# Attention, gated products and soft routing on one core: the first score products over 128 rows, with 20 identity products ahead of them

## The chip, the cores and the metric

The kernel runs on one core of a Trainium2 chip. The metric is device time in microseconds (us) of one execution; smaller is better. The comparison is the median of several executions of the kernel before with the same of the changed kernel. One execution of the kernel before was taken with the hardware profiler, and all rows below come from that one.

## The reference, cut to what matters

Three stages follow one another. Attention for 4 x 8 = 32 heads of 576 positions and width 64, with a decay bias and a causal mask; a gated product over the 2304 tokens; and soft routing of all tokens to 32 slots of 8 experts.

```python
scores = q @ k.T / sqrt(64)
bias   = -(cum[:, None] - cum[None, :])          # cum = cumsum(max(s, 0))
scores = where(causal, -1e9, scores + minimum(bias, 0))
x      = softmax(scores) @ v                     # heads side by side: 2304 x 512
g      = ((x @ w1) * (x @ w2)) @ w3 @ w_out      # 2304 x 512
logits = g @ phi                                 # 2304 x 32
# softmax over tokens -> slot inputs -> two expert layers -> softmax over slots -> out
```

The weights w1, w2, w3 and w_out are in float64, and the kernel turns them into float32 from their raw words.

## The kernel before, in words

A head's scores are products of a q tile and a k tile. The rows that are contracted are the 64 of the head plus 4 that carry the decay bias (two parts of the cumulative sum times ones), 68 in all. `ITEMS` has 40 entries: items 0 to 7 are the query tiles 0, 1, 2 (64, 128 and 128 queries, against 64, 192 and 320 keys) of heads 0 to 7, items 8 to 15 the query tiles 3 and 4 of the same heads (448 and 576 keys, the latter in two cuts of 288), and items 16 to 39 all five tiles of heads 8 to 31. `NF32 = 16` items are the first kind: their q and k stand in one float32 tile [128, 2, 576], rows 0 to 63 fetched by `att_fetch`, rows 64 to 67 by `att_prep` (for items 0 and 1 out of the tiles `dec`, L304, for the others out of the scratch `rows_d` in DRAM, L306), and one float32 product over `rows[:68]` (L308) makes a score tile. Each such product is two TensorE instructions with their weight loads. The later items split q and k into a high part and a rest and make two products of the float32r type, one over 128 rows (`qa`), one over 68 (`qb[:68]`).

The tiles of the first 16 items take turns in six places: three tags (`raw`, `qa`, `qb`) of `NRW = 2` buffers each, so item n takes the place of item n - 6.

For each item: scores in `att_scores` (L341 on TensorE, mask and row maximum on VectorE at L344, exponential on ScalarE at L349), `att_norm` (reciprocal on VectorE, multiplication on GpSimd at L362), `att_transpose` (transposes on TensorE at L377 and L391, copies on ScalarE), and for each pair of heads `att_pv` (products with v, `x_ps`, issued through the helper at L110). `glu_half` (L439, `gl`) makes the gated products over the finished columns of x. Between these steps the float64 words are fetched (L178) and converted (L186 to L201, and GpSimd at L218), three buffers deep.

The program's steps are woven by hand (`att_steps`, `weave`). SyncE issues nearly all DMAs, strictly in the order written. On the other engines a planner with a model of time (`schedule_with_timeline_sim=True`, L1114) puts the instructions in order when the program is built; on the chip each engine then runs its own order and waits on semaphores. `att_values` (L290) fetches v for a pair of heads into one of two buffers, so it waits until an earlier pair's `x_ps` products have read theirs, and every later fetch of SyncE stands behind it. `ident` is the 128 x 128 identity, made by GpSimd (`make_identity`, L747).

Of the kernel before, what the change touches and what calls it, by code (L numbers as in the profile page):

```python
# [10 lines left out]
F32 = mybir.dt.float32  # L11
# [10 lines left out]
P = 128  # L22
B, H, S, D = 4, 8, 576, 64
# [24 lines left out]
def attn_glu_softmoe_kernel(  # L48
# [14 lines left out]
    nc = tc.nc  # L63
# [16 lines left out]
    def psum(tag, name):  # L80
        return ps.tile([P, 512], F32, tag=tag, name=name, bufs=PB[tag])
# [3 lines left out]
    NRW, SCB, PTB, QAB, VB = 2, 3, 2, 2, 2  # L85
    NF32, NDIR, ND, FAR = 16, 2, 1, 3

    A1, CA, CB1, CB, GB1, GB, GC = 0.6, 8, 16, 26, 8, 16, 24

    LKS = {(0, 1): 8, (1, 0): 0, (1, 1): 4}  # L90

# [27 lines left out]
    ident = cp.tile([P, P], F32, name="ident")  # L119
# [144 lines left out]
    hd = {}  # L264
    ITEMS = [(h, t) for t in ((0, 1, 2), (3, 4)) for h in range(H)] + [(h, (0, 1, 2, 3, 4)) for h in range(H, NH)]

    def att_fetch(n, ap):
        h, tiles = ITEMS[n]
        if h % 2 == 0:
            b, c = divmod(h // 2, H // 2)  # L270
            for blk, (_, nt, own) in enumerate(BLK):
                if own[0] in tiles:
                    x_t[b, blk, c] = xpl.tile([P, 2, nt], F32R, tag=f"x{blk}", name=f"x_{b}_{blk}_{c}", bufs=NX)
        q0, q1 = QT[tiles[0]][0], sum(QT[tiles[-1]])
        tag = ("raw", "qa", "qb")[n % 3] if n < NF32 else "raw"
        raw = ap.tile([P, 2, S], F32, tag=tag, name=f"raw_{n}", bufs=NRW)
        m = 64 if n < NF32 else P
        if q0:
            nc.sync.dma_start(raw[:m, 0, q0:q1], qk[h, 0, :m, q0:q1])
            nc.sync.dma_start(raw[:m, 1, :q1], qk[h, 1, :m, :q1])  # L280
        else:
            nc.sync.dma_start(raw[:m, :, :q1], qk[h, :, :m, :q1].rearrange("n p t -> p n t"))
        hd[n] = dict(raw=raw, q0=q0, q1=q1)
# [9 lines left out]
    def att_prep(n, ap):  # L293
        h, tiles = ITEMS[n]
        t = hd[n]
        raw, q0, q1 = t["raw"], t["q0"], t["q1"]
        if n < NF32:
            rows = raw
        else:
            rows = ap.tile([P, 2, S], F32R, tag="qb", name=f"qb_{n}", bufs=QAB)  # L300
            qa = ap.tile([P, 2, S], F32R, tag="qa", name=f"qa_{n}", bufs=QAB)
        if n < NDIR:
            for a in range(2):
                nc.sync.dma_start(rows[64 + 2 * a : 66 + 2 * a, :, :q1].bitcast(F32), dec[a][h : h + 1, :, :, :q1])  # L304
        else:
            nc.sync.dma_start(rows[64:68, :, :q1].bitcast(F32), rows_d[h].rearrange("a b n t -> (a b) n t")[:, :, :q1])  # L306
        if n < NF32:
            t["mul"] = [rows[:68]]  # L308
            return
        rq, rk, qb = raw[:, 0], raw[:, 1], rows  # L310
        nc.vector.tensor_copy(qa[:, 0, q0:q1], rq[:, q0:q1])  # L311
        nc.scalar.dma_start(qb[0:64, 0, q0:q1].bitcast(F32), qa[0:64, 0, q0:q1].bitcast(F32))
        nc.vector.tensor_copy(qa[:, 1, :q1], rk[:, :q1])
        nc.gpsimd.tensor_tensor(  # L314
            out=qb[0:64, 1, :q1], in0=rk[0:64, :q1], in1=qa[0:64, 1, :q1].bitcast(F32), op=ALU.subtract
        )
        nc.gpsimd.tensor_tensor(  # L317
            out=qa[64:, 0, q0:q1], in0=rq[64:, q0:q1], in1=qa[64:, 0, q0:q1].bitcast(F32), op=ALU.subtract
        )
        t["mul"] = [qa, qb[:68]]  # L320

    def att_scores(n, i, ap):
        t, tiles = hd[n], ITEMS[n][1]
        if i == tiles[0]:
            t["nmax"] = sm.tile([P, 6], F32, tag="nmax", name=f"nmax_{n}")
            t["rsum"] = rsum_t[n % 3]
            if n >= H or n % 2 == 0:
                t["sc"] = ap.tile([P, 1600], F32, tag="sc", name=f"sc_{n}", bufs=SCB)
            else:
                t["sc"] = hd[n - 1]["sc"][:, 800:]  # L330
        nmax, rsum, mul = t["nmax"], t["rsum"], t["mul"]
        q0, r = QT[i]
        W = q0 + r

        r = P
        sc = t["sc"][:, 64 * i * i : 64 * i * i + W]
        cuts = [(0, W)] if W <= 512 else [(0, W // 2), (W // 2, W)]
        for m, (a, z) in enumerate(cuts):
            pp = psum("sg", f"sc_ps_{n}_{i}_{m}")
            for x in mul:  # L340
                nc.tensor.matmul(pp[:r, : z - a], x[:, 0, q0 : q0 + r], x[:, 1, a:z], start=x is mul[0], stop=x is mul[-1])  # L341
            m0 = S - P if i == 0 else S - W + a
            last = m == len(cuts) - 1
            nc.vector.tensor_tensor_reduce(  # L344
                out=sc[:r, a:z], in0=pp[:r, : z - a], in1=hd["mask"][:r, m0 : m0 + z - a], scale=-0.125,
                scalar=3.0e38 if m == 0 else nmax[:r, 5:6], op0=ALU.add, op1=ALU.min,
                accum_out=nmax[:r, i : i + 1] if last else nmax[:r, 5:6],
            )
        nc.scalar.activation(  # L349
            out=sc[:r, :W], in_=sc[:r, :W], func=AF.Exp, bias=nmax[:r, i : i + 1], scale=-1.0,  # L350
            accum_out=rsum[:r, i, 0:1],
        )
# [285 lines left out]
    def att_steps(ap):  # L638

        groups = [[] for _ in range(B + 1)]  # L640
        N = len(ITEMS)
        for n in range(N + 1):
            tiles = ITEMS[n][1] if n < N else ()
            old = [i for i in ITEMS[n - 1][1] if i] if 0 < n <= N else []
            sc = [(0.2 + 0.3 * i, lambda i=i, n=n: att_scores(n, i, ap)) for i in tiles]
            tr = [(0.2 + 0.3 * i, lambda i=i, n=n: att_transpose(n - 1, i, ap)) for i in old]
            norm = [(0, lambda n=n: att_norm(n - 1))] if 0 < n <= N else []
            prep = [(0, lambda n=n: att_values(n + 1, ap))] if n + 1 < N else []
            d = FAR if n + FAR < NF32 else 1 if NF32 <= n + 1 < N else 0
            if d:  # L650
                prep += [(0, lambda m=n + d: att_prep(m, ap))]
            d = FAR + 1 if n + FAR + 1 < NF32 else 2 if NF32 <= n + 2 < N else 0
            if d:
                prep += [(0, lambda m=n + d: att_fetch(m, ap))]
            blks = [k for k in range(2) if BLK[k][2][0] in ITEMS[n - 1][1]]
            pv = [(1.4, lambda n=n, k=k: att_pv(n - 2, k)) for k in blks] if n > 0 and n % 2 == 0 else []
            groups[min(B, max(0, (n - 1) // H))] += [
                *sc[:1], *norm, *sc[1:2], *prep, *sc[2:3], *tr[:1], *sc[3:4], *tr[1:2], *sc[4:], *tr[2:], *pv
            ]
        return groups  # L660
# [78 lines left out]
    with tc.tile_pool(name="att", bufs=1) as ap:  # L739
        phi_sb = ap.tile([P, KC, NS], F32, name="phi_sb")  # L740
        u_sb = ap.tile([P, FC, NS], F32, name="u_sb")
        decay_fetch()
        fetch_words(0, ap)
        att_fetch(0, ap)
        fetch_words(1, ap)
        att_fetch(1, ap)
        make_identity(nc, ident)  # L747
        mask = ap.tile([P, S], F32, name="mask")
# [9 lines left out]
        for n in range(NDIR):  # L758
            att_prep(n, ap)
# [4 lines left out]
        for n in range(NDIR, FAR):  # L764
            att_fetch(n + 1, ap)
            att_prep(n, ap)
# [36 lines left out]
        k = GC - GB  # L803
        steps = steps[GB:]
        run(weave(att[2], weave(steps[:k], prep[CB:]) + steps[k:]))
        for b in range(2, B):
            steps, late = glu_steps(b - 1, late)
            n = len(more) // (B - b)
# [5 lines left out]
    pp = pool("pp", 2, reuse_waits="tile")  # L814

    def big(where, name):
        if where == "w":
            return wp.tile([P, 2048], F32, tag="W", name=name, bufs=NW)
        if where == "t":
            return tp2.tile([P, 2048], F32, name=name)  # L820
        return ep.tile([P, 2048], F32, tag="E", name=name)
# [3 lines left out]
    for i in range(2):  # L825
        t = big("e", f"wo_t{i}").rearrange("p (i c) -> p i c", i=2)
# [3 lines left out]
    for i in range(4):  # L830
        t = big("e", f"w3_t{i}").rearrange("p (i c) -> p i c", i=2)
# [67 lines left out]
    for q in range(4):  # L899
        cols = slice(256 * q, 256 * q + 256)  # L900
        yps = psum(("acc", "sg")[q % 2], f"y_ps_{q}")
        for r in range(2):
            for j in range(4):
                f = 4 * r + j
                nc.tensor.matmul(  # L905
                    yps[32 * j : 32 * j + 32, :256], zt[:, j, NS * r : NS * r + NS], w3_t[f // 2][:, f % 2, cols],
                    start=r == 0, stop=r == 1,
# [7 lines left out]
    for r in range(2):  # L915
        for c in range(2):
            for j in range(4):
                f = 4 * r + j
                nc.tensor.matmul(
                    xp[c][32 * j : 32 * j + 32, :256], yt[:, f], wo_t[f // 4][:, f % 4, 256 * c : 256 * c + 256],  # L920
                    start=r == 0, stop=r == 1,
# [196 lines left out]
```

## Time and profile before

| what | value |
|---|---|
| median of 3 runs | 566.16 us (562.83 to 568.1) |
| the profiled execution, its own time | 565.44 us |
| span of that execution, first to last instruction | 563.6 us |
| mean granted TensorE clock over the span | 0.981 |
| TensorE busy (matmul) | 520.0 us, 92% |
| TensorE weight loads busy | 433.9 us, 77% |
| VectorE, ScalarE, GpSimd busy | 316.2, 310.0, 196.7 us |
| DMA, mean rate over the span | 209 GB/s |

The span is 1.84 us shorter than the execution's own time. PE is TensorE's matmul, PEld its weight load, DVE is VectorE, ACT ScalarE, POOL GpSimd, SP SyncE; SPq rows are DMA issues of SyncE's queue. The granted clock is a share of 2.4 GHz. Shares of busy time are means over stages of different kinds.

### The profile page before, as it was taken

Reading aid. Unit: us, or ns where it says so; the run is one execution under the profiler, and the core shown is the slowest. Engines: PE = TensorE matmul, PEld = TensorE weight load, DVE = VectorE, ACT = ScalarE, POOL = GpSimd, SP = SyncE. Lnnn points to the kernel's source line nnn. Section 1 sums busy time; section 2 is a strip of 40 time slices with the busy share of each in tenths; the row PEclk is TensorE's granted clock in tenths of the full one; section 3 lists DMA queues with packets and bytes.
Section 4 is the critical chain, followed back from the end, with each engine's and each line's share of the span. In section 5 each row is a group of like instructions: output and inputs, shape, how many; then the busy total and the mean of one; then the engine's idle time right before and its main releaser. Section 6 shows DMA issues by size and latency. Waiting matters only on the chain. (4 is left out here: it accounts for less than half of the span.)

```text
span 563.6 us, 11844 instructions
## 1 busy us (share of the span) xinstructions
PE 520.0 (92%) x4288; PEld 433.9 (77%) x4288; DVE 316.2 (56%) x966; ACT 310.0 (55%) x845; POOL 196.7 (35%) x247
## 2 busy tenths in 40 slices
PE   3789899998979999899899999999999999999993
PEld 2566688787768897889889889889988999853452
DVE  7568696889964385736574657446631311243333
ACT  4576586788865675646566567357833321321222
POOL 5475464438745374253354444333210000000000
PEclk9997899999979999999999999999999999999998
DMA  5765966868654173345646563555330999689977
GB/s 157 237 179 178 261 203 215 287 219 261 191 201 119 39 220 109 130 135 179 206 136 213 168 197 104 166 167 172 113 113 1 391 413 381 233 300 421 421 296 244
DMA packets 38809, 118.03 MB, mean 209 GB/s; under 512 B 4224, under 2 KB 10560, under 8 KB 35296
## 3 DMA queue, kind: packets, MB, share of 16 engines
q1 hardware_dynamic: 36832, 113.74, 58.8%
q10 hardware_dynamic: 1920, 3.54, 2.5%
q8 instruction: 34, 0.56, 0.4%
q14 instruction: 23, 0.19, 0.1%
HBM read 102.11 MB, written 11.60 MB: 202 GB/s over the span
## 5 line engine op out<-in xcount | busy, mean ns | idle before, releaser
L439 PE MATMUL gl<-x,w12t 128*128 128x320 f32 (+1 forms) x1536 | 238.3, 304 | 1.3 <-DVE nmax L344 0.7
L439 PEld LDWEIGHTS gl<-x,w12t 128*128 128x128 f32 x1536 | 212.2, 191 | 10.0 <-issue 4.3
L362 POOL TENSOR_SCALAR sc<-sc,rinv 128x64 f32<-128x64 f32 (+4 forms) x160 | 92.4, 594 | 53.9 <-DVE rinv L359 39.2
L349 ACT ACTIVATE sc<-sc,nmax 128x64 f32<-128x64 f32 (+4 forms) x160 | 89.5, 560 | 32.2 <-DVE nmax L344 31.6
L317 POOL TENSOR_TENSOR qa<-raw,qa 64x576 fp32r<-64x576 f32 x24 | 36.5, 1522 | 144.1 <-DVE qa L311 138.3
L344 DVE CUSTOM_DVE_ANT_0 sc<-sc_ps,mask 128x64 f32<-128x64 f32 (+4 forms) x160 | 64.8, 424 | 32.1 <-PE sc_ps L341 29.0
L379 ACT COPY pt<-pt_ps 128x128 f32<-128x128 f32 (+3 forms) x128 | 52.2, 423 | 27.1 <-PE pt_ps L377 16.3
L377 PE MATMUL pt_ps<-ident,sc 128*128 128x128 f32 x320 | 56.8, 288 | 4.9 <-ACT pt L379 2.3
L341 PE MATMUL sc_ps<-qa 128*128 128x64 f32 (+1 forms) x144 | 46.6, 336 | 6.0 <-DVE nmax L344 2.5
L377 PEld LDWEIGHTS pt_ps<-ident,sc 128*128 128x128 f32 x320 | 38.8, 145 | 17.3 <-issue 10.0
L341 PE MATMUL sc_ps<-qb 68*128 68x64 f32 (+1 forms) x144 | 44.2, 310 | 4.2 <-issue 4.2
L110 PE MATMUL x_ps<-pt,v 128*64 128x256 f32 (+1 forms) x384 | 47.5, 353 | 0.0
L445 ACT COPY a<-gl 128x256 f32<-128x256 f32 (+1 forms) x64 | 25.3, 398 | 38.5 <-PE gl L439 34.8
L341 PE MATMUL sc_ps<-raw 68*128 68x288 f32 (+4 forms) x96 | 35.5, 514 | 11.1 <-DMA raw<-rows 9.6
L990 POOL MEMSET ht<- 128x1024 f32 x2 | 1.9, 954 | 107.3 <-DVE ew L894 98.4
L186 ACT ACTIVATE w_w<-raw_w 128x512 f32<-128x512 f32 x32 | 21.6, 676 | 31.6 <-DMA raw_w<-in_w 31.6
L314 POOL TENSOR_TENSOR qb<-raw,qa 64x576 fp32r<-64x576 f32 x24 | 38.2, 1590 | 2.2 <-PE gl L439 0.5
L110 PEld LDWEIGHTS x_ps<-pt,v 128*64 128x64 f32 x384 | 32.0, 138 | 6.7 <-issue 1.0
L341 PEld LDWEIGHTS sc_ps<-qa 128*128 128x128 f32 x144 | 27.7, 192 | 9.1 <-DVE nmax L344 3.5
L427 DVE TENSOR_TENSOR x<-x_ps,x 128x320 fp32r<-128x320 f32 (+1 forms) x32 | 14.0, 455 | 36.2 <-ACT x L426 36.1
L341 PEld LDWEIGHTS sc_ps<-raw 68*128 68x128 f32 x96 | 21.2, 259 | 16.3 <-issue 12.1
L341 PEld LDWEIGHTS sc_ps<-qb 68*128 68x128 f32 x144 | 28.0, 194 | 4.6 <-issue 4.4
(180 smaller groups left out, 785.4 us busy)
## 6 DMA issues: line engine op xcount, KB each, us to landing
ew<-in_ew SPq DMA_DIRECT2D x27, 1024.0 KB
raw_w<-in_w SPq DMA_DIRECT2D x32, 512.0 KB
raw<-in_qk SPq DMA_DIRECT2D x24, 576.0 KB
v<-in_v SPq DMA_DIRECT2D x16, 576.0 KB
raw_w3t<-in_w3t SPq DMA_DIRECT2D x16, 512.0 KB
raw_wot<-in_wot SPq DMA_DIRECT2D x8, 512.0 KB
raw_wo<-in_wo SPq DMA_DIRECT2D x8, 512.0 KB
w_d<-w_w SPq DMA_DIRECT2D x8, 512.0 KB
```

Source lines behind the costliest of these rows:

```text
L110: mm = nc.tensor.matmul(out_, lhs, rhs, start=start, stop=stop)
L186: nc.scalar.activation(out=w, in_=hi.bitcast(F32), func=AF.Copy, scale=F64_SCALE)
L314: nc.gpsimd.tensor_tensor(out=qb[0:64, 1, :q1], in0=rk[0:64, :q1], in1=qa[0:64, 1, :q1].bitcast(F32), op=ALU.subtract)
L317: nc.gpsimd.tensor_tensor(out=qa[64:, 0, q0:q1], in0=rq[64:, q0:q1], in1=qa[64:, 0, q0:q1].bitcast(F32), op=ALU.subtract)
L341: nc.tensor.matmul(pp[:r, : z - a], x[:, 0, q0 : q0 + r], x[:, 1, a:z], start=x is mul[0], stop=x is mul[-1])
L344: nc.vector.tensor_tensor_reduce(out=sc[:r, a:z], in0=pp[:r, : z - a], in1=hd["mask"][:r, m0 : m0 + z - a], scale=-0.125, scalar=3.0e38 if ...
L349: nc.scalar.activation(out=sc[:r, :W], in_=sc[:r, :W], func=AF.Exp, bias=nmax[:r, i : i + 1], scale=-1.0, accum_out=rsum[:r, i, 0:1],)
L362: nc.gpsimd.tensor_scalar(out=sc, in0=sc, scalar1=rinv[:, i : i + 1], scalar2=1.0, op0=ALU.mult, op1=ALU.mult)
L377: nc.tensor.transpose(tp[:, j * P : (j + 1) * P], sc[:, j * P : (j + 1) * P], ident)
L379: t["turned", i] = nc.scalar.copy(out=pt[:, p0 : p0 + step * (i - 1) + 1 : step], in_=tp[:, : i * P].rearrange("p (j q) -> p j q", q=P))
L439: nc.tensor.matmul(acc[:, :nt], w12_t[fc][:, wi, n, kc], x_t[b, blk, kc][:, xi], start=k == 0, stop=k == 3 * KC - 1)
L445: nc.scalar.copy(out=a_sb[:, :nt], in_=acc[:, :nt])
```

## The change

The products of items 0 to 15 read all 128 rows of their tile (`t["mul"] = [rows]`) in place of 68. So that rows 68 to 127 are zero, the six places become six lasting tiles `wide_0` to `wide_5`, made by the new function `rows_of` at the fetches of items 0 to 5; rows 64 to 127 of each are cleared once, by VectorE (even) or GpSimd (odd), and the fetches of rows 64 to 67 come after that. Items 6 to 15 use the same tiles again; nothing else is ever written to rows 68 to 127 of them while they serve these items. And in front of the very first score product, into the same PSUM tile, TensorE makes `IDLE = 20` float32 products of the identity with itself (128 x 128 by 128 columns); the score product then overwrites that tile.

```diff
+    IDLE = 20
...
+    wide = []
+
+    def rows_of(n, ap):
+        k = n % (3 * NRW)
+        if k == len(wide):
+            t = ap.tile([P, 2, S], F32, tag=("raw", "qa", "qb")[k % 3], name=f"wide_{k}", bufs=NRW)
+            (nc.vector, nc.gpsimd)[k % 2].memset(t[64:], 0.0)
+            wide.append(t)
+        return wide[k]
...
-        tag = ("raw", "qa", "qb")[n % 3] if n < NF32 else "raw"
-        raw = ap.tile([P, 2, S], F32, tag=tag, name=f"raw_{n}", bufs=NRW)
+        if n < NF32:
+            raw = rows_of(n, ap)
+        else:
+            raw = ap.tile([P, 2, S], F32, tag="raw", name=f"raw_{n}", bufs=NRW)
...
-            t["mul"] = [rows[:68]]
+            t["mul"] = [rows]
...
             pp = psum("sg", f"sc_ps_{n}_{i}_{m}")
+            if n == i == 0:
+                for _ in range(IDLE):
+                    nc.tensor.matmul(pp[:, :P], ident, ident, start=True, stop=True)
```

## Rows read from the trace of the kernel before

**Rows 1.** Cores: span and mean granted clock; page: the clock in 40 slices of 14.1 us.

```profile
core 0: 563.6 us, clock 0.981
PEclk9997899999979999999999999999999999999998
```

**Rows 2.** Line 341 at 20:30 and 30:36, then all run: count, ns min/median/max, first to last start.

```profile
L341 PEld LDWEIGHTS sc_ps<-raw x23: 285/337/337, 19.7 to 29.3; 68*128 68x128 f32 x23
...
L341 PEld LDWEIGHTS sc_ps<-raw x10: 186/192/337, 32.5 to 35.8; 68*128 68x128 f32 x10
...
L341 PEld LDWEIGHTS sc_ps<-qa x144: 186/190/333, 107.8 to 406.4; 128*128 128x128 f32 x144
...
L341 PEld LDWEIGHTS sc_ps<-qb x144: 186/191/338, 108.0 to 406.6; 68*128 68x128 f32 x144
```

**Rows 3.** Timeline of TensorE's matmuls, 9 to 33 us: start, us, instructions.

```profile
9.61 4.61 PE L341 MATMUL sc_ps<-raw 68*128 68x64 f32 x12 [9.61 <-DMA raw<-rows]
...
19.13 3.54 PE L341 MATMUL sc_ps<-raw 68*128 68x64 f32 x10 [0.35 <-DMA raw<-rows_d]
...
23.10 3.41 PE L341 MATMUL sc_ps<-raw 68*128 68x320 f32 x8
...
26.94 0.43 PE L377 MATMUL pt_ps<-ident,sc 128*128 128x128 f32 x1
27.18 2.66 PE L341 MATMUL sc_ps<-raw 68*128 68x64 f32 x8
29.77 0.67 PE L110 MATMUL x_ps<-ptd,v 128*64 128x64 f32 x3
...
32.18 0.69 PE L377 MATMUL pt_ps<-ident,sc 128*128 128x128 f32 x2
```

**Rows 4.** Stretches of 4 us: PE, PEld, DVE, ACT, POOL busy, clock, DMA share, GB/s.

```profile
24.00:28.00 4.00, 4.00 (x15) 3.25 (x15) 3.15 (x14) 3.27 (x13) 2.20 (x4) 1.00 0.99 288
...
44.00:48.00 4.00, 4.00 (x12) 2.92 (x11) 2.62 (x6) 2.04 (x6) 1.33 (x1) 0.50 0.80 246
48.00:52.00 4.00, 4.00 (x30) 3.15 (x30) 3.96 (x10) 2.42 (x7) 2.73 (x3) 0.72 0.04 14
...
60.00:64.00 4.00, 1.98 (x12) 1.32 (x10) 2.41 (x5) 3.17 (x8) 0.00 (x0) 0.98 1.00 273
64.00:68.00 4.00, 3.93 (x16) 3.21 (x17) 3.93 (x9) 2.89 (x8) 1.93 (x3) 0.59 0.86 207
```

**Rows 5.** Timeline of TensorE's matmuls, 39 to 50 us.

```profile
39.75 1.89 PE L341 MATMUL sc_ps<-raw 68*128 68x448 f32 x6
...
43.25 3.62 PE L341 MATMUL sc_ps<-raw 68*128 68x448 f32 x6 [1.17 <-DVE w_w L193]
...
47.59 1.95 PE L439 MATMUL gl<-x,w12t 128*128 128x320 f32 x6
```

**Rows 6.** SyncE's queue to 170 us: longest waits in total, then two issues.

```profile
SPq L290 <- PE x_ps L110: 16.9, 5, 6.1
...
32.28 0.33 SPq L290 DMA_DIRECT2D v<-in_v  x1
...
51.52 0.33 SPq L290 DMA_DIRECT2D v<-in_v  x1
```

**Rows 7.** GpSimd timeline to 30 us, then its memsets by shape: total us, mean ns.

```profile
2.12 0.28 POOL masks.py:199 TENSOR_SCALAR_AFFINE_SELECT ident<-ident 128x128 f32<-128x128 f32 x1
2.35 2.60 POOL L155 MEMSET rows<- 32x512 f32 x6
...
25.80 1.56 POOL L362 TENSOR_SCALAR sc<-sc,rinv 128x64 f32<-128x64 f32 x3 [4.58 <-ACT sc L349]
...
L990 POOL MEMSET ht<- 128x1024 f32 x2 | 1.9, 954 | 107.3 <-DVE ew L894 98.4 <-PE h_ps L981 8.9
```

**Rows 8.** Timeline of VectorE and ScalarE: two instructions that waited for DMAs.

```profile
2.78 0.86 DVE L148 TENSOR_SCALAR dec<-dec 32x576 f32<-32x576 f32 x1 [1.92 <-DMA dec<-in_s]
...
60.83 0.66 ACT L186 ACTIVATE w_w<-raw_w 128x512 f32<-128x512 f32 x1 [3.87 <-DMA raw_w<-in_w]
```

## Prediction, made before the changed kernel ran

> **What bounds the kernel now.** I began with the cores and the clock. The span is 563.6 us at a mean granted clock of 0.981, and the slices show falls in the fourth, fifth and twelfth [rows 1]. That row reads full speed in the first three slices, which the durations contradict: a score product's weight load takes 337 ns (median) from 19.7 to 29.3 us, and among the ten from 32.5 to 35.8 us the same shape goes from 337 to 186 ns, 192 in the median [rows 2]. So until about 32.5 us TensorE ran at the low one of its two levels, 1.2 of 2.4 GHz; the recorded clock only starts to tell at the first recorded fall.
>
> Next I asked what TensorE did while the clock was low. From 19.13 us it works without a gap: the next idle time of the timeline comes after 32.18 us [rows 3], and in 24 to 28 us it is busy 4.00 of 4.00 us [rows 4]. Up to 29.77 us these are score products over 68 rows and a few transposes; then come the first x products, over 128 rows [rows 3], and about three us later the loads are short. The second low stretch has the same look. At 43.25 us TensorE resumes after 1.17 us of idling, the score products over 68 rows take 3.62 us for six instructions where the six at 39.75 us (same widths: 448, 288 and 288 columns) took 1.89 us, and only the gated products over 128 rows from 47.59 us stand ahead of the return [rows 5]; the stretch 44 to 48 us is at 0.50, 48 to 52 us at 0.72 [rows 4].
>
> Who suffers: SyncE. Its fetches of v wait for the x products, 16.9 us in five waits up to 170 us, the longest 6.1, and the two issues at 32.28 and 51.52 us end such waits [rows 6]. Behind them stand all later fetches. In 48 to 52 us the DMA engines are busy 0.04, in 24 to 28 us 0.99 and in 60 to 64 us 1.00 [rows 4]. So this stage alternates: saturated DMA, then DMA standing still until a slow TensorE lets a buffer go. A faster TensorE shortens the second kind, not the first.
>
> **The change part by part.** *Width.* Rows cost no time by themselves: a weight load of the later items takes 190 ns over 128 rows and 191 over 68 [rows 2]. The 96 score instructions stay 96.
>
> *Clock, first stretch.* I take it that score products over 128 rows bring the clock up as x and gated products do, some time after 19.13 us. What is then late? On TensorE's queue the transpose at 26.94 us needs GpSimd's multiplication, begun at 25.80 after waiting 4.58 us for ScalarE [rows 3, 7], which itself stood behind saturated DMA (0.99 in 24 to 28 us) [rows 4]; a faster TensorE doesn't move that. From 26.94 to 32.18 us are 5.24 us of TensorE work at the low level. At the high one that is half, 2.6 us saved, if the clock is up by then. Bounds: nothing if it stays low; if GpSimd too came early, half of 23.10 to 32.18 us, 4.5 us. I take 2.6, as the GpSimd row is the nearest.
>
> *Second stretch.* From 43.25 us to the return in 48 to 52 us: the granted 0.72 there is 0.56 x 4 = 2.24 us at half, so the low level ends at 50.24 and has lasted about 7 us [rows 4, 5]. If the clock doesn't fall, 3.5 us are saved; if it falls (the idling of 1.17 us remains, it ended with VectorE's conversion of words) but 128-row scores bring it back halfway, 1.75 us; if nothing changes, 0. I take 2.4, between the first two. The fetch of v at 51.52 us and the DMA engines, idle at 0.04, move with it, so I count it in full.
>
> *Third stretch.* 64 to 68 us at 0.59 is 0.82 x 4 = 3.3 us at half, 1.6 us to gain at most. It follows idling (1.98 of 4.00 us busy) under saturated DMA, when ScalarE waited 3.87 us for words [rows 4, 8]. The change doesn't take that away; I take 0.3, bounds 0 and 1.6.
>
> *The identity products.* 20 x 2 instructions of 128 columns are 5120 columns. At the low level the first 12 score instructions (2 x (64 + 192 + 320) columns for each of two items, 2304) took 4.61 us, 2.0 ns a column; at the high level 2048 columns took 1.89 us, 0.92 ns [rows 3, 5]. So 4.7 to 10.2 us. They can start when `ident` is done, at 2.40 us, or some 1.1 us later if a clearing of GpSimd stands in front [rows 7]: they end between 7.1 and 13.7 us, in the middle about 10.4, against 9.61 us for the first score, which waited for its DMA [rows 3]. At the middle the first score is 0.8 us late and its two items then need 2.1 us in place of 4.61. Early or late, the next scores wait for `rows_d` until 19.13 us [rows 3], a chain of DMAs behind VectorE in which TensorE has no part. I take 0; bounds 0 and 4.1 us late (all at the low level, from 3.5 us).
>
> *The clearings.* Six of 64 x 1152 elements. The nearest row is GpSimd's 128 x 1024 in 954 ns, so 1.1 us each, and for VectorE I take the same [rows 7]. VectorE's first lies in its wait of 1.92 us for `s` [rows 8]. GpSimd's first pushes `ident` and the memsets of 2.35 to 4.95 us by 1.1 us, still before the scores. The others fall among steps with GpSimd waits such as the 4.58 us [rows 7]. SyncE's fetches of rows 64 to 67 now wait for a clearing too, with v, the next q and k and the words queued behind; that wait has ended if the clearing is put where its tile is made, one or more items ahead. I take 0, bounds 0 and 2.2 us (two GpSimd clearings uncovered). Item 16's tiles now take the places of items 12, 13 and 14 instead of 12, 10 and 11; those scores are done by then: 0.
>
> *The order.* The planner builds a new order around 20 products and 6 clearings. No row shows it; the spread of three runs, 5.3 us, gives a scale: 2.6 us either way, 0 taken.
>
> Sum: 2.6 + 2.4 + 0.3 = 5.3 us off the span, 558.3, plus the 1.84 us around it: 560.1, against this execution's 565.44. The median of 566.16 is 0.7 above it; forecast 560, 1.1% below the median. About 1% (5.7 us) is also what a measurement of this kernel can tell from no change, as its three runs spread by 0.9%.
>
> **The rivals.** *All of it (556).* The clock comes up at once and stays: 4.5 + 3.5 + 1.6 = 9.6 us. For it: all three stretches touch the first items. Against: GpSimd and DMA in between.
>
> *Swallowed (564).* The clock rises, but what TensorE saves is waited for elsewhere: words are late at 60.83 us under a DMA share of 1.00 [rows 4, 8], so fetches issued earlier only queue. Then only some 1.5 us are left.
>
> *The rows aren't what matters (566 to 569).* Here the clock follows TensorE's busy time, zeros or not, and nothing comes back; the identity products cost their 0 to 4.1 us. Against it: busy 4.00 of 4.00 us with the loads still at 337 ns [rows 2, 4]. The Trainium skill, "TensorE: Matmul & The Clock Gate", section "What's actually happening", says that the clock is set by how busy TensorE has been lately and speaks of no rows. By that rule the clock should have come up before 29 us in the kernel before; this trace doesn't show that, so I give it little.
>
> *Slower (570).* The identity products stay at the low level to the end, 13.7 us, and hold the first scores for 4.1 us. It decides from the point where the first item's transposes, and with them the first x products at 29.77 us, slip by more than the quicker scores return: then SyncE's fetch of v at 32.28 us and all behind it slip too. For it: TensorE has only 19.13 - 14.22 = 4.9 us between the second item's scores and the third's, filled in part by transposes [rows 3]. Against: the first scores would be quicker if the clock is up.
>
> **How the numbers follow.** Forecast (560) 0.45, of it 0.32 by over 1%; all of it 0.12; swallowed 0.18; rows don't matter 0.12, mostly within 1%, 0.04 slower; slower 0.13. Faster by over 1%: 0.32 + 0.12 = 0.44. Slower by over 1%: 0.04 + 0.13 = 0.17. The rest, 0.39, within 1%. The range takes in the clearings, the order and the second rival, and leaves out half of the best and half of the worst case: 554.5 to 568.5.
>
> **What would show it.** Right: weight loads of the score products at about 190 ns well before 30 us; first x products done by about 29.6 us; the fetch of v 2 to 3 us ahead of 32.28; the second low stretch shorter; the DMA gap of 48 to 52 us smaller. Wrong: loads at 337 ns up to 32 us in spite of 128 rows; the first score after 12 us; SyncE waiting for a clearing; or an early start whose lead is gone by 70 us, with a DMA share near 1.00 in between.

## The result, and the profile after

| | median, us | lowest to highest | runs | profiled execution: span, mean granted clock |
|---|---|---|---|---|
| before | 565.83 | 560.29 to 568.47 | 20 | 563.6 us, 0.981 |
| after | 569.26 | 565.67 to 573.9 | 20 | 567.1 us, 0.978 |

The ratio is 1.0073, 95% interval 1.005 to 1.0096: 4.1 us slower, where 560 was forecast. The profiled execution of after took 568.96 us by itself.

The clock first. The page of after, its row of the clock in 40 slices of 14.2 us:

```profile
PEclk9698999989999999999999999999999999999998
```

It falls in the second, fourth and ninth slices, where before had its falls in the fourth, fifth and twelfth [rows 1]. The weight loads of after's score products, grouped by line and shape (count, total us, mean ns of one, idle time before), first 12 to 20 us:

```profile
L358 PEld LDWEIGHTS sc_ps<-wide 128*128 128x128 f32 x12 | 1.7, 190 | 0.4 <-DMA wide<-rows 0.4
```

The twelve loads of the first two items average 190 ns, the high level of 2.4 GHz; before they were at 337 until 29 us [rows 2]. But here it was the identity products that had brought the clock up: without them (e1 below) the same twelve products over 128 rows took 4.28 us, with them 2.58. Now TensorE's timeline (start, us, instructions; in brackets idle time and what ended it):

```profile
8.58 6.62 PE L356 MATMUL sc_ps<-ident 128*128 128x128 f32 x40 [8.58 <-POOL ident masks.py:199]
15.04 2.58 PE L358 MATMUL sc_ps<-wide 128*128 128x64 f32 x12
24.32 2.47 PE L358 MATMUL sc_ps<-wide 128*128 128x64 f32 x6 [6.70 <-DMA wide<-rows_d]
...
32.76 0.33 PE L112 MATMUL x_ps<-ptd,v 128*64 128x64 f32 x2
```

The first score starts at 15.04 us instead of 9.61, the third item's at 24.32 instead of 19.13 [rows 3]. TensorE lost 5.4 and 5.2 us before it did anything faster, and the granted clock is 0.50 from 20 to 28 us, through the end of the idling of 6.70 us and the third item's scores. What held it stands on VectorE and GpSimd, timelines from the start:

```profile
1.16 1.02 DVE L275 MEMSET wide<- 64x1152 f32 x1 [0.30 <-issue]
2.37 1.02 DVE L275 MEMSET wide<- 64x1152 f32 x1 [0.19 <-issue]
3.57 1.02 DVE L275 MEMSET wide<- 64x1152 f32 x1 [0.19 <-issue]
4.62 0.85 DVE L150 TENSOR_SCALAR dec<-dec 32x576 f32<-32x576 f32 x1
...
12.33 0.99 DVE L164 TENSOR_SCALAR rows<-rows 32x320 f32<-32x320 f32 x3
```

```profile
0.97 1.05 POOL L275 MEMSET wide<- 64x1152 f32 x1
2.08 0.21 POOL masks.py:197 MEMSET ident<- 128x128 f32 x1
...
3.26 2.78 POOL L157 MEMSET rows<- 32x512 f32 x6
6.09 2.06 POOL L275 MEMSET wide<- 64x1152 f32 x2
8.23 0.29 POOL masks.py:199 TENSOR_SCALAR_AFFINE_SELECT ident<-ident 128x128 f32<-128x128 f32 x1
```

The planner put all six clearings in front. VectorE does three in a row and begins the decay rows at 4.62 us, before 2.78 [rows 8]; GpSimd does three before it finishes `ident` at 8.52, before 2.40, and the six memsets of `rows`, which stood behind `ident`, now stand ahead of it too [rows 7]. The clearings are not all of the late start. VectorE's last decay step (L164) ends at 13.32 us, in the kernel before at 8.51, so 1.84 us of lateness at the first step have become 4.8: the planner put five steps of word conversion (L191 to L195) between the first and the last decay step, where there had been two. `ident` holds none of these steps here. SyncE passes the delay on; its fetches of v (start, us of the issue):

```profile
22.68 0.43 SPq L304 DMA_DIRECT2D v<-in_v  x1
26.76 0.59 SPq L304 DMA_DIRECT2D v<-in_v  x1
34.51 0.33 SPq L304 DMA_DIRECT2D v<-in_v  x1
47.57 0.33 SPq L304 DMA_DIRECT2D v<-in_v  x1
```

The third issued at 32.28 before [rows 6]; it is 2.2 us late. Of the 5.2 us at the third item three had been made up by then, but the fourth is 8 us late again, and the last of the twenty, near 389 us, 3.2 us.

A second thing to see is ScalarE's order. Its timeline in after:

```profile
16.63 0.19 ACT L366 ACTIVATION_READ_ACCUMULATOR sc<-sc,nmax 128x1 f32 x1
20.57 0.66 ACT L188 ACTIVATE w_w<-raw_w 128x512 f32<-128x512 f32 x1 [3.75 <-DMA raw_w<-in_w]
21.13 0.55 ACT L366 ACTIVATE sc<-sc,nmax 128x320 f32<-128x320 f32 x1
```

The scores were finished at 17.62 us, but the third exponential stands behind a conversion of words that waits 3.75 us for its DMA. In the kernel before, the planner had put that conversion (at 15.45 us) behind it (at 13.29). So the edit had two kinds of effect, its own work and a new order of everyone else's, and the experiments had to part them.

### The profile page after: what moved, and what is told of

Its sections match the earlier page's. It is cut to its first block, busy times and chain, and to the rows that moved or that the text cites. A ratio compares the mean times of both kernels' runs of the same rounds, so it can differ in the third digit from the quotient of the medians.

```text
span 567.1 us, 11936 instructions
## 1 busy us (share of the span) xinstructions
PE 517.8 (91%) x4328; PEld 434.3 (77%) x4328; DVE 317.8 (56%) x969; ACT 309.5 (55%) x845; POOL 199.9 (35%) x250
## 4 chain that ended last, share of the span: by engine, by line
PE 40%; DMA 4%; DVE 3%; ACT 1%; issue 1%; POOL 1%; SPq 0%; DVEq 0%; POOLq 0%; ACTq 0%
PE gl L456 18%; DMA raw_w<-in_w 3%; PE x_ps L112 3%; PE o_ps L1036 3%; PE h_ps L998 3%; PE gn_ps L626 2%; PE sc_ps L358 2%; PE pt_ps L394 2%; PE z_ps L112 1%; PE ptd_ps L408 1%; PE y_ps L922 1%; PE lg L112 1%; DVE w_w L200 1%; DMA out<-ot 1%; PE out_ps L1060 1%
## 5 line engine op out<-in xcount | busy, mean ns | idle before, releaser
L394 PE MATMUL pt_ps<-ident,sc 128*128 128x128 f32 x320 | 54.2, 281 | 4.5 <-ACT pt L396 3.9
L394 PEld LDWEIGHTS pt_ps<-ident,sc 128*128 128x128 f32 x320 | 37.5, 142 | 14.8 <-issue 9.7
L358 PE MATMUL sc_ps<-wide 128*128 128x288 f32 (+4 forms) x96 | 29.6, 439 | 10.2 <-DMA wide<-rows_d 7.4
L444 DVE TENSOR_TENSOR x<-x_ps,x 128x320 fp32r<-128x320 f32 (+1 forms) x32 | 14.1, 452 | 32.6 <-ACT x L443 32.4
L366 ACT ACTIVATION_READ_ACCUMULATOR sc<-sc,nmax 128x1 f32 x160 | 30.7, 192 | 0.0
L629 ACT COPY gn<-gn_ps 128x512 f32<-128x512 f32 x40 | 22.5, 584 | 14.1 <-PE gn_ps L626 13.7
```

Source lines behind the costliest of these rows:

```text
L366: nc.scalar.activation(out=sc[:r, :W], in_=sc[:r, :W], func=AF.Exp, bias=nmax[:r, i : i + 1], scale=-1.0, accum_out=rsum[:r, i, 0:1],)
L394: nc.tensor.transpose(tp[:, j * P : (j + 1) * P], sc[:, j * P : (j + 1) * P], ident)
L629: st["turned", blk, k, h] = nc.scalar.copy(out=gn[:r, 4 * h : 4 * h + 4].rearrange("p c f -> p (c f)"), in_=tp[:r])
```

## The experiments

Each group was timed beside its own runs of the kernel before (medians 564.89, 564.95, 564.31, 565.7 and 564.46 us), and differences in us are the ratio's excess times that median. Theory 1: the clearings, in front of the decay rows and `ident`, start all work late, and the clock gives a part back. Theory 2: the identity products stand in the way. Theory 3: the rows leave the clock alone. The theories A to D are named in the expectations of the later groups.

**One part at a time, the planner free.** Of the six clearings alone, the rows go back and no identity products are made:

```diff
-    IDLE = 20
+    IDLE = 0
-            t["mul"] = [rows]
+            t["mul"] = [rows[:68]]
```

Clearings alone (e7_clear_only):

> The changed kernel without its two other parts: the six clearings stay where the planner put them, the products read 68 rows again and there are no identity products. Theory 1 (late start: three clearings stand ahead of the decay rows on VectorE, and item 2's scores come 5 us late; the 128 rows give part of it back through the clock): item 2's scores at about 24 us as in the changed kernel, and nothing given back, so 569 to 573 us, no faster than the changed kernel. Theory 2 (the identity products hold the first scores and that is the loss): 564 to 567 us, like the kernel before.

Clearings and rows, only the first two lines of that diff (e1_no_ident):

> The changed kernel with no identity products; clearings and 128 rows stay. Theory 1 (late start): the first scores come early, but item 2's wait for the decay rows as before, so 567 to 570 us, within 2 us of the changed kernel. Theory 2 (identity products in the way): the loss is gone, 560 to 565 us. Theory 3 (the rows leave the clock alone): no faster than the run with the clearings alone.

The whole change with clearings put elsewhere, one on VectorE and five on GpSimd behind its memsets for the decay rows (e4_clear_late), and the same over 68 rows without identity products (e6_clear_late_rows68):

```diff
-            (nc.vector, nc.gpsimd)[k % 2].memset(t[64:], 0.0)
+            if k == 0:
+                nc.vector.memset(t[64:], 0.0)
...
+        if 0 < n < 3 * NRW:
+            clear(n)
```

> The changed kernel with 128 rows and 20 identity products, but only the first clearing on VectorE; the other five on GpSimd behind its memsets for the decay rows. Theory 1 (late start): item 2's scores back at about 19 us, first x products done by about 30 us, 558 to 563 us. Theory 2 (identity products in the way): still 567 to 570 us. Theory 3 (the rows leave the clock alone): 565 to 567 us, score products at the low level until 32 us.

> The clearings as in the run with late clearings, but products over 68 rows and no identity products: nothing of the change but lasting tiles and clearings off the path. Theory 1: item 2's scores at about 19 us, score loads slow until 32 us, 564 to 567 us, like the kernel before, and 3 to 7 us above the run with late clearings. Theory 3: the same time as the run with late clearings, within 2 us.

Measured: e7 577.96 (ratio 1.0217, 1.0164 to 1.027), e1 571.02 (1.0102, 1.0053 to 1.015), e4 568.97 (1.0076, 1.0041 to 1.0111), e6 580.37 (1.026, 1.0208 to 1.0311). Theory 3 falls: the rows do move the clock, and with them the kernel is 6.5 us faster (e7 to e1). How much of that is theirs these two don't tell, because the planner gave them different orders on all four engines. The weight loads from 29 to 39 us, e1 and then e7:

```profile
L358 PEld LDWEIGHTS sc_ps<-wide 128*128 128x128 f32 x25 | 3.8, 195 | 4.4 <-DVE rinv L376 2.7 <-DVE rinv L375 1.3 <-issue 0.2
```

```profile
L358 PEld LDWEIGHTS sc_ps<-wide 68*128 68x128 f32 x14 | 3.8, 331 | 1.6 <-issue 1.6
```

Theory 2 falls as the main cause: without the identity products nothing is gained. But Theory 1 isn't enough: with the first score at 12.06 us in e4, 3 us earlier than in after, nothing is gained, and e6 is no faster than e7. The orders of the instructions differed in all four from the kernel before and from each other, so the planner's order had to be held.

**TensorE's order held.** The products up to item 10 are chained in the order of the kernel before. Three kernels have cheap clearings: 320 columns of tiles 0 and 1 on VectorE at the start, these columns of the others by ScalarE copies of zeros, the rest on VectorE behind score steps:

```diff
+            if k < 2:
+                nc.vector.memset(t[64:, :, :320], 0.0)
...
+            for e in range(2):
+                nc.scalar.copy(out=raw[64:, e, :320], in_=hd["mask"][64:, :320])
...
+                tc.add_manual_dep(pin[b][0].ins, pin[a][-1].ins.name, order, reason="pin")
```

> The six tiles are kept and their upper rows cleared, but cheaply: for tiles 0 and 1 only the first 320 columns on VectorE at the start, for tiles 2 to 5 these columns by ScalarE copies of zeros, the other columns on VectorE later; score products over 68 rows, no identity products; TensorE's products stand in the order of the kernel before up to item 10. What is left of the change is the cost of clearing. Theory A (the loss is the late start of the decay rows plus the planner's other order of TensorE's work): both are taken away here, so 563 to 568, like the kernel before, and the v fetches at its times within about 1.5 us. Theory B (waiting for clearings as such costs, wherever they stand): about 575.

> The same cheap clearings and the same pinned order, with score products over 128 rows. Theory A (128 rows bring the clock up early; late start and order had swallowed it): 558 to 563, the early low stretch ends by about 20 us, the v fetch that issued at 32.28 us before issues 1 to 3 us earlier. Rival C (a lead at 30 us is lost to the saturated DMA later in any case): 563 to 568, equal to the run over 68 rows, though the fetches up to 50 us lead. Rival B: 568 or more.

> The same with the 20 identity products in front of the first score. If they cost nothing (as the run without them against the changed kernel said): within 2 us of the run without them. If they help by bringing the clock up for the first scores: 1 to 2 us less. If they hold the first scores: 2 to 4 us more.

The changed kernel with nothing but that chain (h1_after_pin):

> The changed kernel with its clearings where they were, and only TensorE's products held in the order of the kernel before up to item 10. Theory A's part on order: the planner's other order puts scores of item 8 ahead of the x products of items 2 and 3, so the fourth v fetch comes 8 us late; with the old order it comes 3 to 5 us late (as the first two), and the time is 563 to 567. Theory B (order costs nothing, the late start is all): 568 to 571 as the changed kernel.

Measured: g3 570.15 (1.0104, 1.005 to 1.0158), g1 565.63 (1.0011, 0.9975 to 1.0047), g2 573.21 (1.0144, 1.01 to 1.0188), h1 569.55 (1.0078, 1.004 to 1.0116). Holding TensorE alone changes nothing in the changed kernel: that part of Theory A falls. In these three the 128 rows are worth 5.3 us (g3 to g1) and the identity products cost 7.5 (g1 to g2), sizes that the next group doesn't bear out; the orders of VectorE, ScalarE and GpSimd differ among these three as well. The cheap clearings with 68 rows should have been as fast as the kernel before and weren't, though the first score is at 9.46 us. TensorE's timeline of g3 shows what is late instead:

```profile
9.46 4.61 PE L390 MATMUL sc_ps<-wide 68*128 68x64 f32 x12 [9.46 <-DMA wide<-rows]
17.79 1.20 PE L429 MATMUL pt_ps<-ident,sc 128*128 128x128 f32 x3 [3.72 <-POOL sc L414]
```

The first transposes wait for GpSimd's multiplication, and come 2.6 us later than at 15.21 us before. Their scores were not late: steps between, on VectorE, ScalarE and GpSimd, stood in another order.

**The order of four engines held.** Nearly every instruction of TensorE, VectorE, ScalarE and GpSimd that the kernel before has is chained in that kernel's order; clearings and identity products are free to fall between, and so is the instruction that finishes `ident`, whose type the chain leaves out (SyncE's order was the same throughout):

```diff
+    for e, places in ORDER.items():
...
+        line = [born[e][k] for k in line]
+        for a, b in zip(line, line[1:]):
+            tc.add_manual_dep(b, a.name, order, reason="as before")
```

With the cheap clearings: 68 rows, 128 rows, 128 rows and identity products; then the changed kernel as it is:

> The same over 68 rows: only the price of clearing is left. Theory D: 564 to 567, like the kernel before. If clearing itself is dear: 568 to 571, as with only TensorE's order held (570.2). The difference to the run over 128 rows is the worth of the rows at an equal order: 3 to 6 us.

> Cheap clearings (tiles 0 and 1: 320 columns on VectorE at the start, tiles 2 to 5: these columns by ScalarE copies of zeros, the other columns on VectorE behind score steps), 128 rows, no identity products, and the whole order of the kernel before on the four engines. Theory D: 556 to 562, first x products by about 28 us (30.4 with only TensorE's order held), v fetch before 31 us. Theory A': 563 to 567, as with only TensorE's order held (565.6). Rival C (a lead is lost to the saturated DMA): 563 to 566, though the fetches up to 50 us lead.

> The same over 128 rows with the 20 identity products. With TensorE's order alone held they cost 7.6 us (573.2 against 565.6), while in the changed kernel taking them out cost nothing. If that was again the order on ScalarE: within 2 us of the run without them. If the identity products cost by themselves, in that the clock falls during the wait for the first transposes behind them: 4 us or more above it.

> The changed kernel, its six clearings and 20 identity products where they were, but every other instruction of TensorE, VectorE, ScalarE and GpSimd held in the order of the kernel before. Theory D (the planner's new order on ScalarE and VectorE is what swallows the gain: in the changed kernel ScalarE's conversion of a word tile at 20.57 us waits 3.75 us for its DMA ahead of exponentials whose scores are there at 17.7 us): without that 560 to 565, in spite of the first score 3 to 5 us late. Theory A' (three clearings ahead of the decay rows, the late start itself): 567 to 571, as the changed kernel.

Measured: j3 563.35 (0.9984, 0.9954 to 1.0015), j1 563.64 (0.9981, 0.995 to 1.0011), j2 565.37 (1.0032, 0.9998 to 1.0065), j4 570.58 (1.0103, 1.007 to 1.0136). Three results. From g3 to j3 nothing changed but the order of the engines' work: 5.9 us slower than before became 0.9 faster, so cheap clearings cost nothing (Theory B falls). In j4 the old order didn't help: Theory D falls for the changed kernel, whose own order was no worse. And at the old start no worth of the 128 rows is seen, j1 against j3: with each ratio uncertain by 0.3%, a gain like the 5.3 us of the forecast would have shown. That contradicts its heart. The identity products, j2 against j1, cost 2.9 us by the ratios and 1.7 by the medians, though the first score starts at 9.61 us in j2 and 9.60 in j1; the intervals overlap. The weight loads of the scores from 23 to 30 us, j1 and j3:

```profile
L382 PEld LDWEIGHTS sc_ps<-wide 128*128 128x128 f32 x14 | 2.5, 225 | 0.5 <-issue 0.5
```

```profile
L382 PEld LDWEIGHTS sc_ps<-wide 68*128 68x128 f32 x16 | 4.6, 336 | 0.8 <-issue 0.8
```

The clock did come up in j1. What then came last stands in j1's timeline of TensorE:

```profile
27.53 0.33 PE L418 MATMUL pt_ps<-ident,sc 128*128 128x128 f32 x1 [1.08 <-POOL sc L403]
...
30.31 0.41 PE L382 MATMUL sc_ps<-wide 128*128 128x64 f32 x2 [1.35 <-DMA wide<-rows_d]
...
32.07 0.37 PE L120 MATMUL x_ps<-ptd,v 128*64 128x64 f32 x1 [1.09 <-ACT ptd L434]
```

and in ScalarE's, where the copy that the x products wait for stands behind three exponentials and a conversion that waited for words:

```profile
29.84 0.67 ACT L198 ACTIVATE w_w<-raw_w 128x512 f32<-128x512 f32 x1 [1.73 <-DMA raw_w<-in_w]
...
31.72 0.30 ACT L434 COPY ptd<-ptd_ps 128x192 f32<-128x192 f32 x1
```

What TensorE saved it spent waiting for GpSimd, for the DMA of rows and for ScalarE, and after that idling the clock fell, under the x products themselves; stretches of 4 us (TensorE, its loads, VectorE, ScalarE, GpSimd busy; granted clock, DMA share, GB/s):

```profile
24.00:28.00 4.00, 2.92 (x15) 1.89 (x15) 3.53 (x13) 3.46 (x12) 1.57 (x4) 0.88 0.97 249
...
32.00:36.00 4.00, 3.87 (x24) 3.25 (x24) 3.65 (x14) 3.53 (x13) 3.07 (x4) 0.60 0.16 31
```

So the fetch of v that was to come 2.6 us earlier issued at 34.28 us in j1, 32.66 in j3.

**The parts of the change at the old order.** The changed kernel's clearings alone (k1) and with 128 rows (k2) are j4 with the first diff, whole or half; k3 is the kernel before with 20 identity products; k4 is j1 with three more memsets on VectorE ahead of the decay rows:

```diff
-                nc.vector.memset(t[64:, :, :320], 0.0)
+                for c in range(4 if k == 0 else 1):
+                    late.append(nc.vector.memset(t[64:, :, : S if c else 320], 0.0))
```

> The six clearings of the changed kernel alone, where it has them, score products over 68 rows, no identity products, all four engines in the order of the kernel before. If the clearings' late start is the loss: 569 to 573 (first score near 15 us, as with the order of the planner), and the v fetches 4 to 6 us late throughout. If the rest of the loss was the planner's order: 564 to 567.

> The same over 128 rows. At the early start and an equal order the rows brought nothing (563.6 against 563.4). If they can't bring anything because the work behind the scores waits for GpSimd, ScalarE and the DMA: within 2 us of the run over 68 rows. If a late start leaves TensorE more behind, so that its clock counts: 3 to 6 us below it.

> The kernel before with 20 identity products alone, its order held. Nothing runs on TensorE before 9.6 us, so they should cost 0 to 2 us (as 565.4 against 563.6 with cheap clearings over 128 rows): 564 to 567. If they cost by themselves, 568 or more.

> The run with cheap clearings, 128 rows and the order of the kernel before (563.6), with three more memsets of 64x1152 (1.02 us each) on VectorE in front of the first decay step: the decay rows and all behind them start some 3 us later, the identity matrix doesn't. If a late start passes through to the end one to one: 566 to 567.5. If it is made up on the way: 563 to 565. If it grows (as 4.5 us seem to have become 7): 568 or more.

Measured: k1 569.74 (1.0118, 1.008 to 1.0156), k2 568.38 (1.0051, 1.0016 to 1.0086), k3 566.17 (1.0007, 0.997 to 1.0044), k4 567.03 (1.0035, 1.0 to 1.007). The clearings alone lose 6.7 us; k1's VectorE shows how:

```profile
4.62 0.85 DVE L158 TENSOR_SCALAR dec<-dec 32x576 f32<-32x576 f32 x1
8.29 0.37 DVE L796 TENSOR_REDUCE rep<-ident 128x32 f32<-128x128 f32 x1 [2.81 <-POOL ident masks.py:199]
```

Two delays stand one behind the other: its three memsets, then 2.81 us for the late `ident`, whose sums stand ahead of the scan in this order. In k1, k2 and j4 that late `ident` is not the work of the clearings alone: its last instruction, which isn't chained, stands behind the memsets of `rows` as in after. In its old place, behind one clearing, it would have been done by about 3.5 us (an estimate: 2.40 plus 1.1), and VectorE asks for it at 5.47. With the late start the rows seem to pay: 3.8 us by the ratios, whose intervals touch at their ends, but 1.4 by the medians (569.74 and 568.38). Stretches of 4 us, k1 and then k2:

```profile
36.00:40.00 4.00, 3.54 (x23) 3.42 (x24) 3.88 (x17) 3.59 (x14) 2.68 (x4) 1.00 0.09 10
40.00:44.00 4.00, 3.87 (x12) 2.61 (x12) 1.99 (x12) 3.10 (x13) 3.31 (x5) 1.00 0.79 232
```

```profile
36.00:40.00 4.00, 3.79 (x23) 2.83 (x20) 3.30 (x13) 3.51 (x13) 3.37 (x4) 0.57 0.30 85
40.00:44.00 4.00, 3.11 (x20) 2.11 (x20) 2.41 (x13) 3.38 (x15) 3.40 (x8) 1.00 0.83 252
```

In k1 TensorE does 12 matmuls in 40 to 44 us, busy 3.87 of 4.00, in k2 20 in 3.11, and the fourth fetch of v issues at 48.46 against 45.20 us. Of these 3.3 us a third is left at the last fetch, at 389.44 against 388.31. (k1's 1.00 is no clock: its first recorded level begins at 49.7 us, and its loads take 335 ns in the median from 36 to 44 us.) Why the rows should pay here and not at the old start stays open. It isn't that words and rows come at their old times and a late TensorE is the last to arrive: SyncE's third fetch of words issues at 15.15 us in both, 10.40 in j3, the third item's first score waits for rows until 24.21 and 24.18 us, 19.48 in j3, and ScalarE's copy holds k2's x products too. k2's TensorE:

```profile
24.18 3.54 PE L366 MATMUL sc_ps<-wide 128*128 128x64 f32 x10 [1.40 <-DMA wide<-rows_d]
...
35.66 0.27 PE L120 MATMUL x_ps<-ptd,v 128*64 128x64 f32 x1 [1.52 <-ACT ptd L418]
```

k3 bears on the early start, with the same view:

```profile
36.00:40.00 4.00, 4.00 (x15) 2.88 (x14) 2.00 (x12) 2.74 (x12) 3.09 (x6) 0.50 0.93 260
...
44.00:48.00 4.00, 3.08 (x14) 2.08 (x13) 3.97 (x10) 2.68 (x8) 1.57 (x1) 1.00 0.89 279
...
64.00:68.00 4.00, 4.00 (x22) 2.59 (x21) 3.86 (x9) 2.98 (x9) 3.17 (x4) 1.00 1.00 266
```

Here TensorE ran at the low level from 15.5 to 42.8 us, ten us past the rise in the profile of before, and the kernel is as fast as before. Its later stretches stay at the high level over 68 rows, where the profile of before had 0.50 and 0.59 [rows 4].

**The clearings divided.** k1 with GpSimd's three behind its memsets for the decay rows, so that `ident` is early (l2); then one on VectorE and five on GpSimd as in e6, at the old order (l1):

```diff
+    for x in cleared:
+        tc.add_manual_dep(x.ins, hd["gp_last"].ins.name, order, reason="clear")
```

> The six clearings alone (68 rows, no identity products), the order of the kernel before, VectorE's three where the change has them, GpSimd's three behind its memsets for the decay rows, so that the identity matrix is early again. If the late identity matrix made most of the loss: 1.8 us late and 565 to 567.5 (against 569.7). If VectorE's three memsets or GpSimd's memsets beside the decay rows made it: 568 to 571.

> The same with one clearing on VectorE (in its wait for s) and five on GpSimd from about 5 to 10.5 us, its idle time. If that place is free: 563 to 566, as the kernel before. If GpSimd's memsets slow VectorE's steps beside them (with the planner's order a 128x2 operation took 2.03 us there, 0.15 in the kernel before): the first score 2 to 3 us late and 566 to 569.

Measured: l2 567.76 (1.0054, 1.0021 to 1.0086), l1 568.17 (1.0033, 0.9994 to 1.0072). By the ratios the late `ident` made 3.7 of the 6.7 us, though the two intervals overlap; the first score comes 2.2 us earlier without it. l1's place was idle time of GpSimd and still no free place. GpSimd and then VectorE of l1:

```profile
5.01 1.06 POOL L290 MEMSET wide<- 64x1152 f32 x1
...
6.52 4.55 POOL L290 MEMSET wide<- 64x1152 f32 x4
```

```profile
5.47 0.67 DVE L809 COPY sel<-rep 128x128 f32<-128x128 f32 x1
5.60 3.01 DVE L169 CAST rows<-dec 32x320 fp32r<-32x320 f32 x3
6.59 2.03 DVE L978 TENSOR_SCALAR part<-part 128x2 f32<-128x2 f32 x1
...
8.94 2.23 DVE L172 TENSOR_SCALAR rows<-rows 32x320 f32<-32x320 f32 x2
```

The same four VectorE groups took 0.20, 0.58, 0.15 and 0.48 us in the kernel before. (The 3.01 and the 2.03 us end together, at 8.61 and 8.62: it is one wait seen twice.) So the first score moved from 9.61 to 12.06 us.

All kernels at the old order, by the start of the first score:

| | rows | first score, us | against before, us |
|---|---|---|---|
| j3 | 68 | 9.60 | -0.9 |
| k3, with identity products | 68 | 9.96 | +0.4 |
| l1 | 68 | 12.06 | +1.9 |
| l2 | 68 | 12.17 | +3.0 |
| k1 | 68 | 14.34 | +6.7 |
| j1 | 128 | 9.60 | -1.1 |
| j2, with identity products | 128 | 9.61 | +1.8 |
| k4 | 128 | 12.61 | +2.0 |
| k2 | 128 | 14.35 | +2.9 |
| j4, with identity products | 128 | 15.78 | +5.8 |

Over 128 rows a late first score costs about its own delay: 3.1 us for 3.01 (j1 to k4), 4.0 for 4.75 (j1 to k2). Over 68 rows it seems to cost more: 2.8 us for 2.46 (j3 to l1), 3.9 for 2.57 (l2), 7.6 for 4.74 (k1). Most of these pairs were measured in different groups, and a single ratio is uncertain by some 2 us.

## Why the prediction was wrong

**The step that failed most** is *The clearings*: "I take 0, bounds 0 and 2.2 us". They cost 6.7 us at the old order by the ratio, 4.0 by the medians (569.74 and 565.7), where 0 was taken. The price of one was right (1.1 us against 1.02 on VectorE, 1.05 on GpSimd). The place was wrong: only "VectorE's first" and "GpSimd's first" were counted in front, the others were to "fall among steps with GpSimd waits". They depend on nothing, and the planner put all six there. VectorE's wait of 1.92 us covers one, not three, and `ident` came 6.1 us later, not 1.1: 3.1 us for three clearings, and nearly all the rest for the memsets of `rows` that the planner moved ahead of it. The prediction's own sign of being wrong came true, the first score after 12 us.

*Width* held: at the high level the loads of 128 rows take the 190 ns of the others. **Clock, first stretch** (2.6) and **second** and **third stretch** (2.4, 0.3). The half about TensorE holds: over 128 rows the loads come down well before 30 us, without the identity products too (j1: 225 ns on the mean of 23 to 30 us, granted clock 0.88 in 24 to 28 us; j3: 336 ns). The rule of the Trainium skill, "TensorE: Matmul & The Clock Gate", section "What's actually happening", that the clock follows how busy TensorE has been, does not tell these cases apart: j3 was busy 4.00 of 4.00 us in every stretch of 4 us from 20 to 40 us, and its score loads still averaged 327 ns from 36 to 42 us (189 from 42.4 to 47 us). Here the measurement decides. The half about the end of the kernel failed. Its question, "What is then late?", was answered with one row of GpSimd; the DMA of rows (1.35 us) and ScalarE's copy behind the words (1.09 us) come last as well, and no gain is seen at the old start (j1 against j3). The later two were priced from one execution: k3 and j3 don't have these falls over 68 rows, and their fifth fetches issue at 51.33 and 51.73 us, before at 51.52 [rows 6]. What holds that fetch in each of them stays open; in the kernel before the profile puts its wait of 6.7 us down to a transpose just behind the x products, not to an x product as the prediction read it. With a late start the rows gave between 1.4 and 3.8 of the 5.3 us in all.

**The identity products**, 0 with a bound of 4.1: alone 0.4 us (k3, -1.7 to +2.5), and 1.7 to 2.9 with 128 rows and the early start (j1 to j2). Behind the late `ident` they hold the first score for 1.4 us (15.78 in j4 against 14.35 in k2), and j4 is 2.9 us above k2, measured beside other runs of before; what they cost is not settled. In the planner's own order the first score waits for its DMA until 15.15 us without them (e1), 15.04 with them, so there they hold nothing. The rival *Slower (570)* named the right time with the wrong culprit: late first scores, but held by the clearings.

**The order**, 0 with 2.6 either way, was the other size that failed: 6.8 us between g3 and j3, 5.6 between e7 and k1, each pair measured beside other runs of before. In the changed kernel as a whole it is not seen to cost anything, though it holds up VectorE's decay steps: 4.1 us slower with its own order, 5.8 with the old one, intervals overlapping. Summed up for the changed kernel by the ratios: clearings +6.7, rows -3.8, identity products up to +2.9, its own order about -1.7; 4.1. These are successive differences, so they add up whatever the single terms are worth, and each is uncertain by 2 to 3 us.

No version here is shown to beat the kernel before; j1 and j3 equal it.

## What to carry to other kernels

A planner may put a preparation that depends on nothing first, as it did here with all six: price it by what stands behind it on its engine at the start, all instances together, not by its own duration or by the wait that would hide the first. A faster engine is worth only the gap to the next thing that arrives, so look for every wait of the same consumer (here for GpSimd, a DMA and a ScalarE copy, 1.1 to 1.4 us each), and ask whether a low clock in one profiled execution recurs. When a planner rewrites the order with the edit, hold the order before you blame a part, all of it: it moved some 6 us by itself, and in k1 one instruction left out of the chain let VectorE wait for 2.81 us.

## What the runs showed of the hardware

GpSimd's memsets of 64x1152 hold up VectorE: in l1 the groups beside them took 0.67, 3.01, 2.03 and 2.23 us instead of 0.20, 0.58, 0.15 and 0.48. The Trainium skill, "SBUF — State Buffer", section "Who interferes with whom", says that casts, copies and scalar operations of VectorE can, in their two-port modes, contend with GpSimd for a shared pair of ports, and that the loser waits for the whole instruction. The trace agrees: the copy begun at 5.47 us ends at 6.14, just behind the memset of 5.01 to 6.07. The next wait was longer than one instruction, until 8.61 us beside memsets of 1.14 us on the mean.

An engine made quicker waits more, and its higher clock need not last: in j1's profile TensorE idled 3.5 us in three waits between 26 and 32.1 us, and the granted clock of the next 4 us was 0.60.
